# Engine choice left to the order tables for some forty copies, casts and scalings, and the tables made anew, in a fused linear-attention and feed-forward kernel

## The chip, the cores and the metric

The kernel runs on one core of one Trainium2 chip. A core has TensorE (PE in the profile; its weight loads are PEld), VectorE (DVE), ScalarE (ACT), GpSimd (POOL) and SyncE (SP), which only issues DMAs here. The metric is the device time of one execution in microseconds (us), lower is better.

## The reference

Blockwise linear attention with a decay per head, and behind it a feed-forward layer with an activation of its own. B, H, S, D = 4, 8, 768, 64.

```python
for b in range(nb):                                   # blocks of 64 positions
    intra = einsum('bhic,bhjc->bhij', qb, kb) * Dmask  # lam ** (i - j), causal
    intra = einsum('bhij,bhjd->bhid', intra, vb)
    inter = einsum('bhid,bhde->bhie', qb * lam_pow, kv_state)
    out[:, :, sl] = intra + inter
    kv_state = lam_block * kv_state + einsum('bhsd,bhse->bhde', kb * rev_pow, vb)
...
x = out.transpose(0, 2, 1, 3).reshape(3072, 512)
h = x @ w_in                                          # 512 x 2048
g = h + sin(alpha * h) ** 2 / (alpha + 1e-9)
result = g @ w_out                                    # 2048 x 512
```

## The kernel before

The attention works on 24 blocks of 128 positions (six to a batch), the feed-forward layer on six chunks c of 512 tokens, four blocks each. All matmuls are in bf16.

**Attention of a block s.** `scale_block` multiplies q by powers of lam (lines L462 and L472 of the profile) and k (L480, L492), and casts v to bf16 (L486, L495). `piece_Q`, `piece_K` and `piece_T` transpose q and k on PE by `ident` into PSUM, and a copy brings them to `qkT` (L516, L539, L543, L571); from block 12 on, SP transposes by DMA instead. `part_S` makes the scores (L612), and DVE multiplies them by the mask into `Sm` (L623). `part_Z` adds the block's k'v to the running state in bank 7 (L648, L656), which is cast to `Zd` or `Zc` (L666, L672). `part_O`, or `piece_P` and `piece_I` in the first four blocks, make the output in PSUM (L694, L707, L716, L759, L779), and a cast writes it to `xT` (L726, L739). `piece_G` joins the scores of one block with the output and state of the block before.

**Feed-forward of a chunk.** `unit_A` (and `unit_A2`, for two parts of half a chunk) makes one of 16 parts m of h in a PSUM bank (L822, L856); ACT takes the sine into `t16` (L832, L866); ACT or POOL squares it into `u16` (L836, L837; L870, L871); DVE adds it to h with 1/alpha into `gT` (L839, L874), which frees the bank. From chunk 2 on, parts rotate through banks 4, 5 and 6. In chunks 0 and 1 `unit_B` multiplies gT by w_out (L887), and an osb copy (L901) goes before the store. In chunks 2 to 5 the second product goes by seven products instead of eight (`unit_P`, L975): `weight_sums` make sums of quarters of w_out once (L930), `token_sums` sums of quarters of gT for each chunk (L953), and `finish` combines the products (copies into `kept`, L1012; sums L1015 and L1021).

**The head.** SP loads lam, q, k and v of the first four blocks, then the first quarter of w_in (`ws`). POOL's queue loads the rest of w_in (`w1`) and w_out, once the second v block has landed. Meanwhile DVE, POOL and ACT make the exponents, `identf`, `ident` and the masks; POOL also clears `Zd` (L427). PE runs unused matmuls (`spin`, L1134 of the profile) on a constant tile until there is something to do.

**The order.** Nothing runs by the order in which the code stands. Each call of `op` records one operation with a number, what it reads and writes, and its engine, or a choice of engines. `_Plan.ORDER` holds, for each engine, the numbers in the order in which that engine issues them; in PE's table a pair (n, columns) stands for n unused matmuls. `_settle` gives an operation to the engine whose table names it:

```python
o = self.ops[table[0]]
assert o.given == e or e in (x[0] for x in o.given)
...
o.eng = e
```

`emit` then puts in the semaphore waits. Two operations of one engine need a wait between them only if `_ordered` says no: if one reads what the other wrote, on any engine but PE. So the tables alone set the order of every engine's queue, and the durations written in the code have no effect on what is issued.

Operations that the prediction names by number: 47 and 48, the casts of the first two v blocks; in the stretch of the sums, the parts gT of chunk 2, part 13, and of chunk 3, part 10.

Of the kernel before, what the change touches and what calls it, by code (L numbers as in the profile page):

```python
# [6 lines left out]
ACTF = mybir.ActivationFunctionType  # L7
# [6 lines left out]
class _Op:  # L14


    def __init__(self, eng, emit, dur, reads, writes, dma, after, issue, lat, runs=64):
        self.eng, self.emit, self.dur = eng, emit, dur
        self.given = eng
        self.issue, self.lat, self.runs = issue, lat, runs  # L20
        self.lag = 2.9 if eng == "POOL" else 2.0
        self.lead = 0
        self.reads, self.writes, self.dma = reads, writes, dma
        self.port = False
        self.after = after
        self.deps = set()
        self.needed = False
        self.count = None
        self.start = None
        self.done = None  # L30
        self.knows = None


class _Plan:
# [17 lines left out]
        ),  # L52
        "ACT": (
# [16 lines left out]
        ),  # L70
        "DVE": (
# [14 lines left out]
        ),  # L86
        "POOL": (
# [7 lines left out]
        ),  # L95
# [67 lines left out]
    def _ordered(d, o):  # L163


        if d.eng != o.eng or d.dma is not None:
            return False
        return d.eng == "PE" or not (set(d.writes) & set(o.reads) or set(d.reads) & set(o.writes))

    def emit(self):  # L170
        order = self._settle()
        place = {o: i for i, o in enumerate(order)}
        for o in order:
            for d in o.deps:
                d.needed = d.needed or not self._ordered(d, o)
# [33 lines left out]
def bass_lightning_attn__then__act_snake_kernel(  # L209
# [35 lines left out]
    QD = ((0, 0), (0, 2), (1, 0), (1, 2))  # L245

    es = contextlib.ExitStack()
    with es:
# [55 lines left out]
        def _(_unused_eng):  # L304
# [76 lines left out]
            def cast_w1_first():  # L381
                for lo in (0, 256):
                    op("DVE",
# [3 lines left out]
            def load_w2(i, after):  # L387
# [26 lines left out]
                fill=1.0, base=0, channel_multiplier=1), 0.5, ["identf"], ["identf", "select"])  # L414
            op("DVE", lambda e: e.tensor_copy(ident[:, :], identf[:, :]), 0.2, ["identf"], ["ident"])
            op("DVE", lambda e: e.memset(maskf[:, :, :], 1.0), 0.3, writes=[("maskf", i) for i in range(3)])
            for i in range(3):
                t, ks = (4, 2) if i < 2 else (2, 1)
                for r in ((0, 64), (64, 128)) if i < 2 else ((0, 128),):
                    op("POOL", lambda e, i=i, r=r, t=t, ks=ks: e.affine_select(  # L420
# [825 lines left out]
```

## Time and profile before

| | |
|---|---|
| three runs | 210.68, 211.11, 211.37 us; median 211.11 |
| span of the profiled execution | 209.8 us |
| around the span (median less span) | 1.3 us |
| PE, DVE, ACT, POOL busy | 97, 76, 76, 60% of the span |
| DMA | 33.35 MB, mean 159 GB/s |
| first product with w_in (L856) starts | 18.99 us |

The profiled execution has no other time of its own on its page than its span. Busy shares count an engine's time from the start to the end of its instructions; the ends of matmuls are modelled. The chain is the work that ended last, followed back from the end. In the windows the first number of an engine is its busy time in the stretch, the (x) its instructions, then come the granted clock of PE (1.00 is full), the DMA share and GB/s.

### The profile page before, as it was taken

To read this page: it belongs to the slowest core of one execution; us is meant where nothing else is said; L and a number is where in the kernel's file an instruction comes from. 1 tells how busy PE (TensorE), PEld (TensorE's weight loads), DVE (VectorE), ACT (ScalarE), POOL (GpSimd) and SP (SyncE) were. 2 spreads that over 40 slices of the span, in tenths; PEclk is the share of its full clock that TensorE was granted. 3 is DMA by queue.
4 is the path that set the end of the run, shared out by engine and by line. 5 is a ranking of instruction groups with operands and counts; after the bars stand their busy time and mean duration, and the time that the engine had idled before them with its cause. 6 is when DMAs were issued, how large, how long until landed. Compare 5 with 4: busy or idle time off the path is not lost.

```text
span 209.8 us, 4867 instructions
## 1 busy us (share of the span) xinstructions
PE 203.5 (97%) x1975; PEld 134.3 (64%) x1975; DVE 160.3 (76%) x266; ACT 158.7 (76%) x294; POOL 126.9 (60%) x130
## 2 busy tenths in 40 slices
PE   7979999999999999999998999999999999999995
PEld 6847444457677776555555667766667765666894
DVE  4884557563999866868899799889698699777643
ACT  4949995968998989999997887787963889568210
POOL 7075354994469578679885392944581957378300
DMA  4999999999998999999999920190000004000514
GB/s 141 310 318 232 206 213 237 246 229 256 220 264 205 227 245 230 223 233 196 246 271 228 213 53 0 33 271 2 3 0 3 0 23 179 3 0 0 200 40 163
DMA packets 78998, 33.35 MB, mean 159 GB/s; under 512 B 55408, under 2 KB 76160, under 8 KB 78976
## 3 DMA queue, kind: packets, MB, share of 16 engines
q1 hardware_dynamic: 73744, 27.14, 56.2%
q0 software_dynamic: 3696, 3.67, 10.5%
q10 hardware_dynamic: 1536, 2.24, 3.3%
q8 instruction: 15, 0.25, 0.5%
q14 instruction: 7, 0.06, 0.1%
HBM read 27.28 MB, written 6.29 MB: 160 GB/s over the span
## 4 chain that ended last, share of the span: by engine, by line
PE 83%; DVE 6%; DMA 3%; SPq 3%; ACT 2%; issue 1%
PE bank L822 27%; PE bank L975 22%; PE bank L887 13%; PE bank L856 10%; DMA v<-in_v_dram 3%; PE bank L716 3%; SPq L315 3%; PE bank L612 3%; DVE gT L839 2%; PE bank L694 1%; DVE Sm L623 1%; PE bank L511 1%; PE bank L656 1%; DVE w L930 1%; PE bank L534 1%; PE bank L707 1%
## 5 line engine op out<-in xcount | busy, mean ns | idle before, releaser
L822 PE MATMUL bank<-xT,w 128*128 128x512 bf16 x296 | 70.5, 379 | 0.0
L839 DVE SCALAR_TENSOR_TENSOR gT<-u,rinv,bank 128x512 bf16<-128x512 bf16 x74 | 53.6, 742 | 18.2 <-ACT u L836 12.5
L832 ACT ACTIVATE t<-bank,alpha 128x512 bf16<-128x512 f32 x74 | 50.0, 684 | 21.0 <-PE bank L822 20.5
L822 PEld LDWEIGHTS bank<-xT,w 128*128 128x128 bf16 x296 | 28.3, 98 | 28.4 <-DVE gT L839 0.4
L836 ACT ACTIVATE u<-t 128x512 bf16<-128x512 bf16 x59 | 36.5, 628 | 1.3
L837 POOL TENSOR_TENSOR u<-t 128x512 bf16<-128x512 bf16 x15 | 16.0, 1066 | 34.1 <-ACT t L832 30.5
L953 POOL TENSOR_TENSOR gT<-gT 128x512 bf16<-128x512 bf16 x24 | 27.8, 1172 | 11.2 <-DVE Xs L953 6.0
L623 DVE TENSOR_TENSOR Sm<-bank,mask 128x1024 bf16<-128x1024 f32 x24 | 29.1, 1218 | 4.3 <-PE bank L648 1.8
L887 PE MATMUL bank<-w,gT 128*128 128x512 bf16 x128 | 31.4, 380 | 0.0
L874 DVE SCALAR_TENSOR_TENSOR gT<-u,rinv,bank 128x256 bf16<-128x256 bf16 x44 | 18.8, 476 | 7.8 <-ACT u L870 6.1
L472 POOL TENSOR_TENSOR qk<-q,Lq 128x512 bf16<-128x512 f32 x20 | 21.2, 1075 | 2.8 <-DMA q<-in_q_dram 2.8
L856 PE MATMUL bank<-xT,w 128*128 128x256 bf16 x176 | 22.2, 273 | 0.0
L492 POOL TENSOR_TENSOR qk<-k,Lk 128x512 bf16<-128x512 f32 x20 | 20.9, 1053 | 0.6 <-DMA k<-in_k_dram 0.6
L866 ACT ACTIVATE t<-bank,alpha 128x256 bf16<-128x256 f32 x44 | 18.9, 476 | 2.0 <-PE bank L856 1.5
L887 PEld LDWEIGHTS bank<-w,gT 128*128 128x128 bf16 x128 | 11.7, 98 | 12.2
L856 PEld LDWEIGHTS bank<-xT,w 128*128 128x128 bf16 x176 | 16.4, 98 | 3.5 <-issue 0.3
L953 POOL TENSOR_TENSOR Xs<-gT 128x512 bf16<-128x512 bf16 x13 | 16.1, 1235 | 1.5 <-DVE gT L839 1.4
L975 PE MATMUL bank<-w,gT 128*128 128x256 bf16 (+1 forms) x136 | 16.3, 266 | 0.0
L975 PE MATMUL bank<-w,Xs 128*128 128x256 bf16 (+1 forms) x136 | 16.0, 267 | 0.1
L975 PE MATMUL bank<-ws,gT 128*128 128x256 bf16 x128 | 15.8, 273 | 0.0
L975 PEld LDWEIGHTS bank<-w,gT 128*128 128x128 bf16 x136 | 12.6, 98 | 3.2
L975 PEld LDWEIGHTS bank<-w,Xs 128*128 128x128 bf16 x136 | 12.4, 98 | 2.8 <-DVE osb L1021 0.3
(101 smaller groups left out, 276.0 us busy)
## 6 DMA issues: line engine op xcount, KB each, us to landing
q<-in_q_dram SPq DMA_DIRECT2D x12, 512.0 KB, 6.2
k<-in_k_dram SPq DMA_DIRECT2D x24, 256.0 KB, 5.5
v<-in_v_dram SPq DMA_DIRECT2D x24, 256.0 KB, 5.4
out_dram<-osb SPq DMA_DIRECT2D x14, 256.0 KB, 2.5
w<-in_moe_w_out_dram POOLq DMA_DIRECT2D x4, 512.0 KB, 11.4
w<-in_moe_w_in_dram POOLq DMA_DIRECT2D x3, 512.0 KB, 9.0
ws<-in_moe_w_in_dram SPq DMA_DIRECT2D x2, 512.0 KB, 7.5
out_dram<-osb ACTq DMA_DIRECT2D x8, 128.0 KB, 4.0
```

The lines of the kernel that those rows point to most:

```text
L472: lambda e, a=a: e.tensor_tensor(qk2[:, j:j + 2, 4 * a:4 * a + 4, :], q32[:, jq, 4 * a:4 * a + 4, :, :].rearrange("p h t d -> p t h d"), b ...
L492: lambda e: e.tensor_tensor(qk2[:, j, H:2 * H, :], block32(k32, jl), lk, ALU.mult), 1.05,
L623: op("DVE", lambda e: e.tensor_tensor(Sm[js][:, :, :], banks[:, 512 * b0:512 * b0 + 1024].rearrange("p (c i) -> p c i", i=128), bass.AP(ma ...
L822: ins = e.matmul(ps[hb][:, c0:c1], w1[:, kc, 128 * m:128 * (m + 1)], xT[x][:, kc, c0:c1], start=(kc == 0 and c0 == lo), stop=(kc == NKC - ...
L832: op("ACT", lambda e: e.activation(t16[ju][:, w], ps[hb][:, w], ACTF.Sin, scale=alpha[:, m:m + 1]), 0.69 if hi - lo == TCH else 0.475, [ba ...
L836: lambda e: (e.activation(u16[ju][:, w], t16[ju][:, w], ACTF.Square) if e is nc.scalar else e.tensor_tensor(u16[ju][:, w], t16[ju][:, w], ...
L839: op("DVE", lambda e: e.scalar_tensor_tensor(out=gT[g][:, m, w], in0=u16[ju][:, w], scalar=rinv[:, m:m + 1], in1=ps[hb][:, w], op0=ALU.mul ...
L856: ins = e.matmul(ps[hb][:, 256 * i:256 * i + 256], w1[:, kc, 128 * (m + i):128 * (m + i + 1)], xT[x][:, kc, lo:lo + 256], start=(kc == 0 a ...
L866: op("ACT", lambda e, i=i: e.activation(t16[ju][:, 256 * i:256 * i + 256], ps[hb][:, 256 * i:256 * i + 256], ACTF.Sin, scale=alpha[:, m + ...
L887: ins = e.matmul(ps[ob][:, w], gT[g][:, m, 128 * s4:128 * (s4 + 1)], w2[:, m, w], start=(m == 0), stop=(m == NM - 1),)
L953: e.tensor_tensor(dst, in0, in1, alu), 0, rd, wr))
L975: ins = e.matmul(ps[ob][:, lo + d0:lo + d1], lhs, rhs[:, d0:d1], start=first and p == 0, stop=(p == NM // 2 - 1), skip_group_check=True)
```

## The change

Four edits.

1. Operations that had a fixed engine, or a choice of two, now name a set: `AD` is ACT or DVE, `DP` is DVE or POOL, `ADP` all three. These are the scalings of q and k, the v casts, the copies to qkT, the casts to Zd and xT, the first w1 casts, the osb copies and two copies in `finish`.
2. All five tables are made anew. On the way 35 more operations leave ACT than come to it (291 to 256), DVE goes from 266 to 292 and POOL from 119 to 128. SP's loads and the order of PE's units change too.
3. The unused matmuls are others: before the first transposes 42 of 112 columns and 30 of 128 become 7 of 512, 24 of 128, 2 of 512 and 41 of 128; later ones, of 128 and 512 columns between the first real matmuls, become 6 of 128 in one place.
4. POOL's small fills lose the shared key `select` that kept them in order. Instead, two neighbours in POOL's table get a wait between them if one of them is a mask fill over 64 partitions. And the four Exp instructions read `warm`, so that they follow the first one.

```diff
@@ class _Op
+        self.some = False
+        self.strict = None
@@ _Plan.ORDER, the first entries
         "PE": (
-            (42,112), 39, (30,128), 57, (11,128), 55, (1,128), 53, (1,128), 59, (8,128), 61, (1,512), 62,
-            (3,512), 65, 67, 69, 70, (3,512), 73, 75, 78, 80, 82, 85, (2,512), 87, 90, 91, 93, 124, 130, 140,
+            (6, 512), (1, 512), (24, 128), (2, 512), (9, 128), (32, 128), 59, 57, 39, 55, 53, 61, 62, 67, 69,
+            70, 65, 78, 75, (6, 128), 73, 82, 80, 85, 87, 90, 93, 91, 124, 130, 140, 136, 147, 144, 151, 159,
...
         "POOL": (
-            12, 13, 14, 18, 15, 21, 22, 24, 25, 27, 29, 30, 50, 47, 48, 102, 103, 52, 105, 106, 104, 142, 107,
+            21, 14, 24, 12, 13, 15, 41, 22, 25, 18, 27, 45, 50, 47, 48, 29, 30, 102, 52, 103, 105, 104, 106,
...
         "SP": (
-            0, 2, 3, 4, 5, 6, 7, 8, 9, 10, 11, 96, 97, 112, 109, 110, 111, 113, 114, 116, 115, 117, 119, 118,
+            0, 2, 3, 5, 4, 6, 7, 9, 8, 10, 11, 96, 97, 109, 110, 112, 111, 113, 114, 115, 117, 116, 118, 122,
...
@@ _ordered, emit
-        if d.eng != o.eng or d.dma is not None:
+        if d.eng != o.eng or d.dma is not None or d is o.strict:
             return False
...
+        last = None
+        for o in order:
+            if o.eng == "POOL" and o.dma is None:
+                if last is not None and (o.some or last.some):
+                    o.strict = last
+                    o.deps.add(last)
+                last = o
@@ constants
-    QD = ((0, 0), (0, 2), (1, 0), (1, 2))
+    AD = (("ACT", 0, 0), ("DVE", 0, 0))
+    DP = (("DVE", 0, 0), ("POOL", 0, 0))
+    ADP = (("ACT", 0, 0), ("DVE", 0, 0), ("POOL", 0, 0))
@@ scale_block (q, k, v; the same in four more places)
-                    ported(op("POOL",
+                    ported(op(DP,
                        lambda e, a=a: e.tensor_tensor(
                            qk2[:, j:j + 2, 4 * a:4 * a + 4, :],
...
-                ported(op((("ACT", 0.62, 0.0), ("POOL", 1.05, 0.3)) if s > 11 else "ACT",
+                ported(op(ADP,
                    lambda e: (e.copy if e is nc.scalar else e.tensor_copy)(v2[:, j, :, :], block32(v32, jl)), 0.62,
@@ part_Z
-                        op("ACT" if s < NP else (("ACT", 0.36, 0.0), ("DVE", 0.43, 0.0)), lambda e, r=r: ...
+                        op(AD, lambda e, r=r: ...
@@ unit_B, finish
-                op("ACT", lambda e: e.copy(osb[jo][:, w], ps[ob][:, w]), 0.59, [bank(ob)], parts)
+                op(AD, lambda e: (e.copy if e is nc.scalar else e.tensor_copy)(osb[jo][:, w], ps[ob][:, w]), 0.59, [bank(ob)], parts)
```

More of the change, by code (lines that the diff above doesn't have):

```diff
@@ L382, in cast_w1_first @@
                 for lo in (0, 256):
-                    op("DVE",
+                    op(AD,
                        lambda e, lo=lo: (e.copy if e is nc.scalar else e.tensor_copy)(
@@ L413, in _ @@
                 out=identf[:, :], in_=identf[:, :], pattern=[[-1, 128]], compare_op=ALU.not_equal,
-                fill=1.0, base=0, channel_multiplier=1), 0.5, ["identf"], ["identf", "select"])
+                fill=1.0, base=0, channel_multiplier=1), 0.5, ["identf"], ["identf"])
             op("DVE", lambda e: e.tensor_copy(ident[:, :], identf[:, :]), 0.2, ["identf"], ["ident"])
@@ L419, in _ @@
                 for r in ((0, 64), (64, 128)) if i < 2 else ((0, 128),):
-                    op("POOL", lambda e, i=i, r=r, t=t, ks=ks: e.affine_select(
+                    part = op("POOL", lambda e, i=i, r=r, t=t, ks=ks: e.affine_select(
                         out=maskf[r[0]:r[1], i, :], in_=maskf[r[0]:r[1], i, :], pattern=[[1, t], [t, 128 // t]],
                         compare_op=ALU.is_ge, fill=0.0, base=-i if i < 2 else 0, channel_multiplier=-ks), 0.3,
-                       [("maskf", i), "select"], [("maskf", i), "select"])
+                       [("maskf", i)], [("maskf", i)])
+                    part.some = i < 2
                 op("DVE", lambda e, i=i: e.tensor_copy(mask[i][:, :], maskf[:, i, :]), 0.2, [("maskf", i)], [("mask", i)])
             for i in range(2):
-                op("POOL", lambda e, i=i: e.memset(Zd[i][:, :, :], 0.0), 0.5, writes=[("Zd", i, 0), ("Zd", i, 1), "select"])
+                op("POOL", lambda e, i=i: e.memset(Zd[i][:, :, :], 0.0), 0.5, writes=[("Zd", i, 0), ("Zd", i, 1)])
             op("ACT", lambda e: e.activation(lnlam[:, :], lam_bc[:, :], ACTF.Ln), 0.25, ["lam"], ["lnlam"])
@@ L434, in _ @@
             op("ACT", lambda e: e.activation(Lq[:, NB:NB + 4, :], lnL[:, 2 * NB:2 * NB + 4, :], ACTF.Exp), 0.2,
-               ["lnL"], ["Lq4"])
+               ["lnL", "warm"], ["Lq4"])
             op("ACT", lambda e: e.activation(Lp[:, :, :], lnL[:, 0:NP, :], ACTF.Exp, scale=-1.0), 0.2,
-               ["lnL"], ["Lp"])
+               ["lnL", "warm"], ["Lp"])
             op("ACT", lambda e: e.activation(Lk[:, :, :], lnL[:, NB:2 * NB, :], ACTF.Exp, scale=-1.0), 0.3,
-               ["lnL"], ["Lk"])
-            op("ACT", lambda e: e.activation(Lq[:, 0:NB, :], lnL[:, 0:NB, :], ACTF.Exp), 0.2, ["lnL"], ["Lq"])
+               ["lnL", "warm"], ["Lk"])
+            op("ACT", lambda e: e.activation(Lq[:, 0:NB, :], lnL[:, 0:NB, :], ACTF.Exp), 0.2, ["lnL", "warm"], ["Lq"])
             op("ACT", lambda e: e.activation(warm[:, :], lnlam[:, 0:1], ACTF.Sin, scale=0.0), 1.5,
@@ L446, in _ @@
             op("ACT", lambda e: e.copy(alpha[:, :], ps[4][:, 0:NM]), 0.2, [bank(4), "warm"], ["alpha"])
-            def QE(s, a):
-                return "DVE" if (s, a) in QD else "POOL"
             def ported(o):
@@ L460, in scale_block @@
                         for t in (0, 2):
-                            ported(op(QE(a, t),
+                            ported(op(DP,
                                lambda e, a=a, t=t: e.tensor_tensor(
@@ L467, in scale_block @@
                                    ALU.mult),
-                               1.05 if QE(a, t) == "POOL" else 0.64,
+                               0.64,
                                [("q32", a, 0), ("q32", a, 1), "Lq4"], [("q2", t, a), ("q2", t + 1, a)]))
                 for a in range(2) if s % 2 == 0 and s > 2 else ():
-                    ported(op("POOL",
+                    ported(op(DP,
                        lambda e, a=a: e.tensor_tensor(
@@ L478, in scale_block @@
                     for a in range(2) if s % 2 == 0 else ():
-                        eng, dur = ("DVE", 0.68) if s + a < 3 else ("POOL", 1.05)
-                        ported(op(eng, lambda e, a=a: e.tensor_tensor(
+                        ported(op(DP, lambda e, a=a: e.tensor_tensor(
                             qk2[:, j:j + 2, H + 4 * a:H + 4 * a + 4, :],
@@ L483, in scale_block @@
                             bass.AP(Lp, n * H + 4 * a, [[NP * H, 128], [H, 2], [1, 4], [0, D]]), ALU.mult),
-                           dur, [("k32", jl + a), "Lp"], [("k2", j, a), ("k2", j + 1, a)]))
+                           0.68, [("k32", jl + a), "Lp"], [("k2", j, a), ("k2", j + 1, a)]))
                     for a in range(2) if s % 2 == 0 else ():
-                        ported(op("ACT" if s and not a else "POOL", lambda e, a=a: (e.copy if e is nc.scalar else e.tensor_copy)(
+                        ported(op(ADP, lambda e, a=a: (e.copy if e is nc.scalar else e.tensor_copy)(
                             v2[:, j:j + 2, 4 * a:4 * a + 4, :],
@@ L490, in scale_block @@
                     return
-                ported(op("POOL",
+                ported(op(DP,
                    lambda e: e.tensor_tensor(qk2[:, j, H:2 * H, :], block32(k32, jl), lk, ALU.mult), 1.05,
                    [("k32", jl), "Lk"], [("k2", j, 0), ("k2", j, 1)]))
-                ported(op((("ACT", 0.62, 0.0), ("POOL", 1.05, 0.3)) if s > 11 else "ACT",
+                ported(op(ADP,
                    lambda e: (e.copy if e is nc.scalar else e.tensor_copy)(v2[:, j, :, :], block32(v32, jl)), 0.62,
@@ L538, in piece_Q @@
                     if len(tbs) == 2:
-                        op("ACT", lambda e, a=a: e.copy(qkT[:, jt:jt + 2, 2 * a:2 * a + 2, :], tps[a]),
+                        op(AD, lambda e, a=a: (e.copy if e is nc.scalar else e.tensor_copy)(
+                            qkT[:, jt:jt + 2, 2 * a:2 * a + 2, :], tps[a]),
                            0.59, [bank(tbs[a])], [("qT", jt, a), ("qT", jt + 1, a)])
@@ L569, in piece_K @@
                 for t in range(2):
-                    op("ACT" if s else (("DVE", 0.43, 0.0), ("ACT", 0.6, 0.0)),
+                    op(AD,
                        lambda e, t=t: (e.copy if e is nc.scalar else e.tensor_copy)(qkT[:, jt + t, 4:8, :], tps[t]),
@@ L665, in then @@
                         r = slice(64 * h, 64 * h + 64)
-                        op("ACT" if s < NP else (("ACT", 0.36, 0.0), ("DVE", 0.43, 0.0)), lambda e, r=r: (e.copy if e is nc.scalar else e.tensor_copy)(
+                        op(AD, lambda e, r=r: (e.copy if e is nc.scalar else e.tensor_copy)(
                             Zd[s % 2][r, :, r], ps[ZB][r, :].rearrange("p (a b) -> p a b", b=128)[:, :, r] if s < NB else
@@ L737, in evict @@
                 P.lead = -20
-                for eng, a0, a1, dur in (("ACT", 0, 2, 0.46), ("DVE", 2, 4, 0.4)) if len(obs) > 1 else (("ACT", 0, 4, 0.74),):
-                    op(eng, lambda e, a0=a0, a1=a1: (e.copy if e is nc.scalar else e.tensor_copy)(
+                for a0, a1 in ((0, 2), (2, 4)) if len(obs) > 1 else ((0, 4),):
+                    op(AD, lambda e, a0=a0, a1=a1: (e.copy if e is nc.scalar else e.tensor_copy)(
                         xT[c % RX][:, a0:a1, BL * i4:BL * (i4 + 1)].rearrange("p a (u x t) -> p a u t x", u=nq // 2, t=2),
                         ps[obs[a0 // 2 % len(obs)]][:, 128 * a0:128 * a1].rearrange(
-                            "p (a u t x) -> p a u t x", a=a1 - a0, u=nq // 2, t=2)), dur,
+                            "p (a u t x) -> p a u t x", a=a1 - a0, u=nq // 2, t=2)), 0.4,
                        [bank(obs[a0 // 2 % len(obs)])], [("xT", c % RX, i4, a) for a in range(a0, a1)])
@@ L1011, in finish @@
                 if i in (1, 3):
-                    op("ACT", lambda e: e.copy(c1 if i == 1 else ny, got), 0.59 if n == 2 else 0.37, [bank(ob)], kc if i == 1 else kn)
+                    op(AD, lambda e: (e.copy if e is nc.scalar else e.tensor_copy)(c1 if i == 1 else ny, got), 0.59, [bank(ob)], kc if i == 1 else kn)
                     return
```

103 rows, old and new, of the table ORDER are left out of this document.

## The prediction

> **What bounds the kernel now.** I read the page first: the busy shares, then the chain that ended last.
>
> ```profile
> span 209.8 us, 4867 instructions
> PE 203.5 (97%) x1975; PEld 134.3 (64%) x1975; DVE 160.3 (76%) x266; ACT 158.7 (76%) x294; POOL 126.9 (60%) x130
> PE 83%; DVE 6%; DMA 3%; SPq 3%; ACT 2%; issue 1%
> ```
>
> TensorE is the bound: it is on the chain for 83% of the span. The change leaves all its useful matmuls alone, so it can only win or lose where TensorE waits. Next I asked the windows where that is. The columns are the engines' busy us in each stretch.
>
> ```profile
> 105.00:110.00 5.00, 5.00 (x29) 2.65 (x27) 5.00 (x6) 4.58 (x9) 4.42 (x4) 1.00 1.23 274
> 110.00:115.00 5.00, 4.44 (x53) 2.97 (x51) 4.87 (x8) 3.85 (x7) 3.19 (x3) 1.00 1.04 228
> 120.00:125.00 5.00, 4.89 (x47) 3.21 (x46) 5.00 (x8) 4.03 (x8) 5.00 (x6) 1.00 0.38 71
> ```
>
> Between 20 and 205 us these last two are the only windows of 5 us in which PE is not 5.00 busy: 0.56 + 0.11 = 0.67 us. In both DVE is full (4.87 and 5.00), and so it is just before (5.00). The ends of matmuls are modelled, so shorter gaps are hidden in "5.00"; still, most of the chip time behind 20 us is already TensorE's work, and no reordering can give much there. The chain in order of time shows who held TensorE at 112 us:
>
> ```profile
> 104.76 1.23 DVE Sm L623
> 105.99 1.31 DVE gT L839 x2
> 107.30 1.19 DVE Xs L953
> 108.49 0.66 DVE gT L839
> 109.15 1.88 DVE w L930
> 111.05 0.43 DVE Zd L666
> ...
> 112.32 0.40 PE bank L694 x4
> ```
>
> For 7.5 us the chain is DVE's queue alone. It is the stretch in which weight sums (L930) and token sums (L953) are added to the ordinary work. DVE, not ACT, is what is nearly late today.
>
> The chain's first part is the head: the load of v, then ACT's short evictions one behind the other, up to the first product with w_in (L856).
>
> ```profile
> 4.16 1.13 POOL L427 MEMSET Zd<- 128x512 bf16 x2
> 5.84 2.50 DVE L462 TENSOR_TENSOR qk<-q,Lq 128x512 bf16<-128x512 f32 x4 [1.01 <-ACT Lq L434]
> 7.20 0.40 PE L534 MATMUL bank<-ident,qk 128*128 128x128 bf16 x4 [0.18 <-DVE qk L462]
> 13.61 0.62 POOL L486 CAST v<-v 128x512 bf16<-128x512 f32 x1 [1.31 <-DMA v<-in_v_dram]
> 14.29 0.62 PE L648 MATMUL bank<-v,qk 64*128 64x128 bf16 x8 [0.90 <-POOL v L486]
> 15.01 0.75 ACT L666 CAST Zd<-bank 64x256 bf16<-64x256 f32 x2
> 18.99 2.07 PE L856 MATMUL bank<-xT,w 128*128 128x256 bf16 x16
> ```
>
> **The change part by part.** *Which engine does what.* By the two sets of tables, ACT goes from 291 to 256 instructions (table loads apart), DVE from 266 to 292, POOL from 119 to 128. These rows price the moves:
>
> ```profile
> L472 POOL TENSOR_TENSOR qk<-q,Lq 128x512 bf16<-128x512 f32 x20 | 21.2, 1075 | 2.8 <-DMA q<-in_q_dram 2.8
> L462 DVE TENSOR_TENSOR qk<-q,Lq 128x512 bf16<-128x512 f32 x4 | 2.5, 688 | 1.0 <-ACT Lq L434 1.0
> L495 ACT CAST v<-v 128x512 bf16<-128x512 f32 x19 | 11.6, 618 | 0.0
> L901 ACT COPY osb<-bank 128x512 f32<-128x512 f32 x8 | 4.7, 589 | 0.1
> L1021 DVE TENSOR_TENSOR osb<-bank,kept 128x512 f32<-128x512 f32 x6 | 4.1, 684 | 0.5 <-PE bank L975 0.5
> L839 DVE SCALAR_TENSOR_TENSOR gT<-u,rinv,bank 128x512 bf16<-128x512 bf16 x74 | 53.6, 742 | 18.2 <-ACT u L836 12.5 <-POOL u L837 5.2
> ```
>
> Ten q and k scalings go POOL to DVE: 10 x 0.69 = 6.9 us onto DVE, 10 x 1.05 off POOL. Eighteen v casts leave or change places, twelve of them ACT to POOL (0.62 each) and six onto DVE; no row has that cast on DVE, so I bound it from below by half a scaling (0.35) and above by a whole one (0.69), and take 0.4: 2.4 us. Eight output and kept copies go ACT to DVE; by L1021 as the nearest read of PSUM on DVE they cost 0.68 each, less for two halves, about 5 us. Eighteen squares go ACT to POOL and fourteen come back. Small evictions mostly exchange, net about 3 us onto DVE; weight sums move three from DVE to POOL (-2 us). DVE ends some 14 us heavier (168 to 182 us of summed durations), ACT some 20 lighter, POOL 8 heavier. So the change relieves the engine that TensorE does not wait for and loads the one that it does wait for. ACT's relief I cost at nothing: the chain gives ACT 2%, nearly all in the head.
>
> *What DVE and POOL share.* Rows of the timeline, DVE first and then POOL, the durations of one form (min, median, max), and line L953 alone in one window:
>
> ```profile
> 107.22 1.27 DVE L953 TENSOR_TENSOR Xs<-gT 128x512 bf16<-128x512 bf16 x1
> 109.07 1.95 DVE L930 TENSOR_TENSOR w<-w 128x1024 bf16<-128x1024 bf16 x1
> ...
> 107.05 1.16 POOL L953 TENSOR_TENSOR gT<-gT 128x512 bf16<-128x512 bf16 x1
> 108.17 2.30 POOL L930 TENSOR_TENSOR w<-w 128x1024 bf16<-128x1024 bf16 x1
> ...
> L953 DVE TENSOR_TENSOR gT<-gT x24: 409/418/1372, 98.2 to 200.2; 128x512 bf16<-128x512 bf16 x24
> 97.50:128.20 30.70, 7.15 (x11) 8.31 (x7) 1.00 0.92 193
> ```
>
> A token sum takes DVE 0.41 us at best and up to 1.37. The one that started at 107.22 ended 0.28 us after POOL's (107.05 + 1.16 = 108.21): it stood still until POOL was through, then ran. The weight sum at 109.07 did the same behind POOL's 2.30. The last row is line L953 alone: eleven DVE sums took 7.15 us where 11 x 0.41 = 4.5 would do. [...]
>
> *The stretch of the sums.* One product of four matmuls is 3.45 / 4 = 0.86 us:
>
> ```profile
> 35.53 3.45 PE bank L822 x16
> ```
>
> I compare the same two DVE instructions in both orders: gT of chunk 2, part 13, and gT of chunk 3, part 10. Before, 28 DVE instructions lie between them (17.9 us), with 21.6 us of TensorE work between their matmuls. After, 39 lie there (25.1 us): 13 of L839, 11 token sums, 3 masks, 3 weight sums, 3 scalings or v casts, 3 Zd, 3 others; and TensorE has 13 + 4 + 8 products of about 0.87 and some 3.4 us of attention by the starts of its matmuls, 25.1 us. DVE instructions overlap a little (two of L839 take 1.31 on the chain, not 2 x 0.74), 0.09 each: 25.1 - 39 x 0.09 = 21.6 us, so 3.5 us are over for waiting. Seventeen of the 39 read two SBUF tensors or cast from SBUF. At the stretch of the rows above, (7.15 - 4.5 + 1.27) over 14 sums = 0.28 each, they lose 17 x 0.28 = 4.8 us: DVE is 1.3 us late. The low end is 0 (POOL happens to be elsewhere). The high end: POOL is busy three quarters of the time and a DVE sum meets the middle of a 1.16 us one, 0.75 x 0.58 x 17 = 7.4, so 3.9 late. I take 1.3, the row's, against the 0.6 lost there before: net +0.7, from -0.6 to +3.3. Behind each late gT stands a bank of the three (4, 5, 6) that the next products rotate through, so DVE's lateness reaches TensorE within about two products.
>
> *The 55 to 75 us stretch.* [...] Cost +0.2, from 0 to 1.
>
> *The head.* SP loads the second half of v before the first, but POOL casts the first half first (ops 47, 48). Both now wait for the fourth load, which let the row at 13.61 go. So the second cast ends at 13.61 + 2 x 0.62 = 14.85 and the first state product (L648) starts 0.56 later than 14.29. Behind the casts POOL clears Zd (0.6 each, 1.13 for both, at 4.16 before): done at 15.4 and 15.9, and the Zd casts that began at 15.01 need the first at 15.4: no more than 0.1 beyond the 0.56. From there ACT has the same Zd pair to do twice, but half the third pair and one xT go to DVE. The last waits are ACT's xT evictions, as before. I take +0.6 (18.99 to 19.6), from -0.4 (the evictions moved to DVE shorten ACT's row) to +1.5. On the way there TensorE has 74 unused matmuls in a row where it had 72 before its first transpose, and identf is made on POOL behind a q scaling of 1.05, so the first transposes come at about 9 us and not 7.20. [...] The POOL queue's weight loads slide too, by 1.8 us behind casts and clears; before them SP no longer sends a k block, so the engines have the same bytes to move less that block: 0, at most +1.
>
> *POOL's own waits* between neighbours that touch half the partitions, and Exp's wait on the warm-up, are some 0.1 us each before 9 us, under the loads. *The tail* from the last product on is the same chain: 0.
>
> **Sum.** +0.6 + 0.7 + 0.2 = +1.5 us. The page's span is 209.8 and the median of the three runs 211.1, so 1.3 us lie around the span; the forecast is 211.1 + 1.5 = 212.6 us. I hold 0.3%, 0.6 us, to be the least that a measurement of this kernel tells from no change.
>
> **Rivals.**
> *DVE fits, the order is simply better (faster).* If POOL's sums happen to lie beside DVE's one-input work, the 0.67 us at 110 to 125 go and the head gains its 0.4: 211.1 - 0.67 - 0.4 = 210.0. For it: only 0.67 us was lost with DVE full, so the orders do fit. [...] Chance 0.21.
> *A wash.* The head costs 0.6 and the sums give 0.6 back: 211.1. Chance 0.15.
> [...] The high ends: 3.3 at the sums, 1 at 55 to 75 us, 1 in the head: 216.4. [...] Chance 0.16.
> *TensorE slow again in the head.* The first 42 unused matmuls (112 columns) took longer per column than the next 30 (128 columns):
>
> ```profile
> 1.52 3.55 PE L1134 MATMUL bank<-Xs 128*128 128x112 bf16 x42 [1.52 <-DVE Xs L410]
> 5.16 1.85 PE L1134 MATMUL bank<-Xs 128*128 128x128 bf16 x30
> ```
>
> That is 84.5 ns against 61.7, or 0.75 ns a column against 0.48. Nearly all unused matmuls now lie before 9 us; between 9 and 19 only six are left, so TensorE idles more. If it fell back for as long as at the start, 3.55 us of work would take 1.3 us more: 212.6 + 1.3 = 213.9. [...] The gaps I see are under 2 us. Chance 0.08.
>
> The forecast itself has 0.40.
>
> **How the numbers follow.** Faster takes the first rival, 0.21, and a little of the wash's lower half, 0.22. Same is most of the wash and the forecast's low edge, 0.16. Slower is the rest, 0.62. The range leaves out the best tenth and the worst tenth: 210.2 to 216.0.
>
> **What would show it.** Right: PE below 5.00 in several windows between 98 and 130 us, the chain there on DVE L839 and on sums whose durations pass 1 us; first L856 at 19.6; ACT near 138 us busy, DVE near 175. The term for the head is wrong if L856 starts before 19; the term for the sums is wrong if PE stays 5.00 through 100 to 130 with DVE full. [...]

## The result, and the profile after

| | before | after |
|---|---|---|
| median, us | 211.17 (210.68 to 211.37, 4 runs) | 227.91 (227.64 to 228.63, 4 runs) |
| ratio, 95% interval | | 1.0802 (1.0771 to 1.0833) |
| span of the profiled execution, us | 209.8 | 225.9 |
| first product with w_in (L856, now L864) starts | 18.99 | 24.74 |

Slower, as forecast, but by 16.7 us and not by 1.5, outside the range. Medians are over all executions; a ratio leaves out those more than 1.5% above the fastest of the same kernel. Lines of the kernel after stand 7 to 11 further down than before (L839 is L847, L953 is L961, L930 is L938).

The page of after, the lines that answer to those shown of before, and the granted clock in 40 slices:

```profile
span 225.9 us, 4816 instructions
PE 206.6 (91%) x1927; PEld 134.8 (60%) x1953; DVE 184.0 (81%) x292; ACT 141.7 (63%) x259; POOL 139.8 (62%) x139
PEclk9985799999999999999999999999999999999999
PE 58%; DVE 26%; ACT 8%; POOL 2%; issue 2%; DMA 1%; ACTq 0%; DVEq 0%; POOLq 0%
```

TensorE is on the chain for 58% instead of 83%, DVE for 26% instead of 6%. The granted clock dips in the third to fifth slices (0.8, 0.5, 0.7), most in the fourth. The windows show both kinds of loss; the columns are as in the prediction's:

```profile
10.00:15.00 5.00, 2.64 (x44) 1.91 (x45) 4.97 (x11) 1.64 (x4) 4.42 (x6) 1.00 1.17 307
15.00:20.00 5.00, 4.81 (x78) 3.66 (x76) 3.89 (x4) 2.32 (x5) 4.57 (x7) 0.51 1.01 187
20.00:25.00 5.00, 5.00 (x90) 3.94 (x89) 1.94 (x4) 3.09 (x7) 0.00 (x0) 0.50 1.17 188
120.00:125.00 5.00, 4.45 (x50) 2.84 (x48) 5.00 (x6) 4.03 (x8) 5.00 (x4) 1.00 1.05 235
125.00:130.00 5.00, 2.79 (x17) 1.49 (x16) 4.91 (x6) 2.34 (x6) 5.00 (x5) 1.00 1.01 165
130.00:135.00 5.00, 3.82 (x24) 2.19 (x24) 5.00 (x8) 2.68 (x5) 4.31 (x4) 1.00 0.29 65
```

First loss: for about 10 us, from 15.2 to 25.4 us, TensorE ran at half its clock (granted clock 0.50 in that stretch), and the first product with w_in came 24.74 - 18.99 = 5.75 us late. Second loss: behind that product the kernel needs 225.9 - 24.7 = 201.2 us, before 209.8 - 19.0 = 190.8, so 10.4 us more. By the starts of the matmuls TensorE stands for 0.44 and 0.89 us at 45 and 46 us, 0.89 at 103, 0.71, 2.08, 0.82, 0.28 and 1.64 between 122 and 136, 1.12 at 146, 0.99 at 157 and some smaller ones. The chain in order of time at the longest of these; then the timeline of DVE and of POOL at the same place; then DVE's groups (us in all and mean ns):

```profile
120.94 1.45 DVE w L938
122.39 0.66 DVE gT L847
123.05 0.64 DVE gT L961
123.69 2.53 DVE w L938
126.21 0.66 DVE gT L847
```

```profile
123.61 2.60 DVE L938 TENSOR_TENSOR w<-w 128x1024 bf16<-128x1024 bf16 x1
...
123.37 2.30 POOL L938 TENSOR_TENSOR w<-w 128x1024 bf16<-128x1024 bf16 x1
125.63 1.49 POOL L499 TENSOR_TENSOR qk<-k,Lk 128x512 bf16<-128x512 f32 x1
```

```profile
L961 DVE TENSOR_TENSOR gT<-gT 128x512 bf16<-128x512 bf16 x25 | 17.9, 724 | 0.1
L961 DVE TENSOR_TENSOR Xs<-gT 128x512 bf16<-128x512 bf16 x19 | 12.0, 637 | 0.1
L480 DVE TENSOR_TENSOR qk<-q,Lq 128x512 bf16<-128x512 f32 x8 | 7.2, 902 | 0.0
L938 DVE TENSOR_TENSOR w<-w 128x1024 bf16<-128x1024 bf16 x3 | 4.8, 1603 | 0.0
```

A weight sum that takes DVE 0.68 us (the shortest of the three here, and their mean in e5) took 2.60: POOL's, begun 0.24 earlier, ended at 125.67, and DVE was through 0.54 later. The gT behind it (126.21) frees the bank that TensorE waits for. Over the four groups DVE spends 41.9 us; at 0.41 for a token sum, 0.69 for a scaling and 0.68 for a weight sum it would be 25.6.

### The profile page after: what moved, and what is told of

Read it like the earlier page. It is cut to its first block, busy times and chain, and to the rows that moved or that the text cites. A ratio compares the mean times of both kernels' runs of the same rounds, so it can differ in the third digit from the quotient of the medians.

```text
span 225.9 us, 4816 instructions
## 1 busy us (share of the span) xinstructions
PE 206.6 (91%) x1927; PEld 134.8 (60%) x1953; DVE 184.0 (81%) x292; ACT 141.7 (63%) x259; POOL 139.8 (62%) x139
## 3 DMA queue, kind: packets, MB, share of 16 engines
q0 software_dynamic: 3696, 3.67, 10.4%
q10 hardware_dynamic: 1536, 2.24, 3.5%
## 4 chain that ended last, share of the span: by engine, by line
PE 58%; DVE 26%; ACT 8%; POOL 2%; issue 2%; DMA 1%; ACTq 0%; DVEq 0%; POOLq 0%
PE bank L830 16%; PE bank L983 12%; PE bank L895 9%; PE bank L864 9%; DVE gT L847 8%; DVE gT L961 3%; ACT t L840 3%; DVE Xs L961 3%; PE bank L620 3%; ACT u L844 3%; PE bank L724 2%; DVE Sm L631 2%; DVE qk L480 2%; DVE w L938 2%; PE bank L656 2%
## 5 line engine op out<-in xcount | busy, mean ns | idle before, releaser
L830 PE MATMUL bank<-xT,w 128*128 128x512 bf16 x280 | 69.0, 380 | 7.9 <-DVE gT L847 6.5
L847 DVE SCALAR_TENSOR_TENSOR gT<-u,rinv,bank 128x512 bf16<-128x512 bf16 x74 | 53.3, 740 | 11.8 <-ACT u L844 7.2
L830 PEld LDWEIGHTS bank<-xT,w 128*128 128x128 bf16 x296 | 27.3, 98 | 37.7 <-DVE gT L847 10.5
L845 POOL TENSOR_TENSOR u<-t 128x512 bf16<-128x512 bf16 x22 | 23.1, 1058 | 25.4 <-ACT t L840 23.5
L844 ACT ACTIVATE u<-t 128x512 bf16<-128x512 bf16 x52 | 32.4, 629 | 2.9 <-DVE gT L847 0.8
L961 POOL TENSOR_TENSOR gT<-gT 128x512 bf16<-128x512 bf16 x23 | 29.0, 1273 | 7.9 <-DVE Xs L961 4.0
L895 PE MATMUL bank<-w,gT 128*128 128x512 bf16 x118 | 29.7, 379 | 1.5 <-ACT qkT L523 0.7
L499 POOL TENSOR_TENSOR qk<-k,Lk 128x512 bf16<-128x512 f32 x18 | 20.3, 1136 | 4.9 <-PE bank L664 4.9
L864 PE MATMUL bank<-xT,w 128*128 128x256 bf16 x176 | 22.6, 276 | 0.0
L961 POOL TENSOR_TENSOR Xs<-gT 128x512 bf16<-128x512 bf16 x13 | 16.2, 1248 | 6.8 <-DVE gT L847 6.8
L895 PEld LDWEIGHTS bank<-w,gT 128*128 128x128 bf16 x128 | 11.9, 98 | 12.5 <-DMA w<-in_moe_w_out_dram 0.6
L864 PEld LDWEIGHTS bank<-xT,w 128*128 128x128 bf16 x176 | 16.6, 99 | 3.4 <-DVE qk L480 0.4
L879 POOL TENSOR_TENSOR u<-t 128x512 bf16<-128x512 bf16 x4 | 4.2, 1038 | 22.5 <-ACT t L874 22.5
L961 DVE TENSOR_TENSOR gT<-gT 128x512 bf16<-128x512 bf16 x25 | 17.9, 724 | 0.1
L983 PE MATMUL bank<-w,gT 128*128 128x256 bf16 (+1 forms) x136 | 15.5, 266 | 0.0
```

What stands on the lines that cost most here:

```text
L499: lambda e: e.tensor_tensor(qk2[:, j, H:2 * H, :], block32(k32, jl), lk, ALU.mult), 1.05,
L830: ins = e.matmul(ps[hb][:, c0:c1], w1[:, kc, 128 * m:128 * (m + 1)], xT[x][:, kc, c0:c1], start=(kc == 0 and c0 == lo), stop=(kc == NKC - ...
L844: lambda e: (e.activation(u16[ju][:, w], t16[ju][:, w], ACTF.Square) if e is nc.scalar else e.tensor_tensor(u16[ju][:, w], t16[ju][:, w], ...
L845: e.tensor_tensor(u16[ju][:, w], t16[ju][:, w], t16[ju][:, w], ALU.mult)), 0,
L847: op("DVE", lambda e: e.scalar_tensor_tensor(out=gT[g][:, m, w], in0=u16[ju][:, w], scalar=rinv[:, m:m + 1], in1=ps[hb][:, w], op0=ALU.mul ...
L864: ins = e.matmul(ps[hb][:, 256 * i:256 * i + 256], w1[:, kc, 128 * (m + i):128 * (m + i + 1)], xT[x][:, kc, lo:lo + 256], start=(kc == 0 a ...
```

## The experiments

**Where: the head or the rest?** Theories: the two losses are separate and add; or the rest is only late because the head is. The changed code took the tables of before, then the head (all up to the first product with w_in) of one kernel and the rest of the other.

```diff
 ORDER = {
-    tables of after
+    e1: tables of before
+    e2: head of before, then what is left of the tables of after
+    e3: head of after, then what is left of the tables of before
```

> The changed code with the five order tables of the kernel before, unused matmuls included. If the loss is in the tables alone, as both theories have it, this is 211.1 us within 0.6. If the lost ordering key of POOL's fills or the Exp's wait on the warm-up cost something, it is above 212.

> Everything up to the first product with w_in in the order and on the engines of before (with its unused matmuls), everything behind it as in the changed kernel. Granted clock 1.00 throughout. If the two stretches add, the head's 5.8 us go and about 10.4 are left over before: 222 us. If the rest was only late because the head was (loads, clock), it is below 216. If the rest has slack that had swallowed part of the head's delay, it is above 223.

> The opposite: the head of the changed kernel, the rest as before. If the two stretches add: 211.1 + 5.8 = 217 us, with the granted clock at half for about 10 us from 15 us on. If the rest takes the delay back: 213 to 215.

e1: 211.72 in one run; in twelve more:

> The changed code with the tables of before, as in the first run, now timed in rounds. If the code edits cost something: 211.5 to 211.9 and a ratio over 1.002. If the first run was a chance value: within 0.2% of before.

210.94, ratio 1.0005 (0.9991 to 1.0018): the code edits cost nothing, the tables are all of it. e2: 224.63, ratio 1.0643 (1.0584 to 1.0703), 2.6 over the forecast; a stall of 2.32 us at 31 us, where the two orders meet, is its own. The stalls of the rest stand as in after, in the same places and sizes (2.08, 0.82, 0.28, 1.64, 1.12, 0.99), although the clock was full (1.00) in the profiled execution: the second loss is the rest's own. e3 gave no single time: four executions from 216.7 to 227.4 us. The fastest is near the 217 that adding would give, the others are not, so the sum isn't tested there. Its longest execution is the one in the profile, and this is what DVE and then POOL did in it from 38 to 49 us:

```profile
39.55 9.49 DVE L939 TENSOR_TENSOR Ta<-w 128x1024 bf16<-128x1024 bf16 x1
48.96 1.39 DVE L848 SCALAR_TENSOR_TENSOR gT<-u,rinv,bank 128x512 bf16<-128x512 bf16 x2
...
38.30 1.05 POOL L500 TENSOR_TENSOR qk<-k,Lk 128x512 bf16<-128x512 f32 x1
39.31 2.04 POOL L481 TENSOR_TENSOR qk<-q,Lq 128x512 bf16<-128x512 f32 x2
41.31 1.03 POOL L500 TENSOR_TENSOR qk<-k,Lk 128x512 bf16<-128x512 f32 x1
42.31 4.17 POOL L939 TENSOR_TENSOR ws<-w 128x1024 bf16<-128x1024 bf16 x2
46.45 2.03 POOL L481 TENSOR_TENSOR qk<-q,Lq 128x512 bf16<-128x512 f32 x2
48.45 2.48 POOL L500 TENSOR_TENSOR qk<-k,Lk 128x512 bf16<-128x512 f32 x2
```

One weight sum of 0.7 us stood for 9.49 us, behind seven POOL instructions without a gap, until 48.48, and TensorE stood for 6.83 us. Six of POOL's instructions ended without letting it in; at the seventh end it went, though POOL did not pause there: its next two scalings, begun at 48.45, took 2.48 us where two take 2.1. What made the seventh end different is not shown. It is a single event: in the twenty profiles here 383 sums, scalings and v casts of DVE's from 18 us on waited 0.1 us or more for POOL, and all the others went at the first end of a POOL instruction. The weight sum and its neighbours in this order are before's; only the head is different.

**The clock.** Theories: TensorE's idling made the chip halve its clock; or the half clock lies beside other waits.

```diff
-    (32, 128), 59, 57, 39, 55, 53, 61, 62, 67, 69, 70, 65, 78, ...
+    (47, 128), 59, 57, 39, 55, 53, 61, (3, 512), 62, (4, 512), 67, (1, 512), 69, 70, 65, (1, 512), 78, ...
```

> The changed kernel with more unused matmuls where TensorE idled between 9 and 16 us: 15 of 128 columns ahead of the first transposes, then 3, 4, 1 and 1 of 512 columns between the transposes and scores. Theory clock (TensorE's idling made the chip halve its clock): granted clock 1.00 throughout, first product with w_in near 21.5 us instead of 24.74, total about 225. Theory late start (the head waits for POOL and DVE anyway, the half clock lies beside other waits): first product no earlier than 23.7, total 227 or more. If the clock is halved all the same, idling is not its cause.

225.41, ratio 1.0672 (1.0637 to 1.0706), so 2.5 us less than after. The windows of e4, and from its timeline the first product with w_in:

```profile
10.00:15.00 5.00, 3.92 (x48) 2.31 (x49) 4.97 (x10) 1.64 (x4) 4.68 (x8) 1.00 1.17 311
15.00:20.00 5.00, 4.52 (x121) 3.40 (x119) 4.76 (x5) 3.16 (x8) 4.02 (x6) 1.00 1.03 201
20.00:25.00 5.00, 4.85 (x70) 3.57 (x72) 2.42 (x4) 3.99 (x10) 0.00 (x0) 1.00 1.17 177
```

```profile
21.79 1.48 PE L867 MATMUL bank<-xT,w 128*128 128x256 bf16 x12
```

The same window of before:

```profile
10.00:15.00 5.00, 3.92 (x85) 2.21 (x86) 4.35 (x6) 2.20 (x5) 2.99 (x4) 1.00 1.16 310
```

Theory clock holds: with TensorE 3.92 busy from 10 to 15 us (2.64 in after, 3.92 before) the clock stays full, and the first product comes 2.95 us earlier. It still comes 2.8 us later than before. In this window 3.65 us busy (e2) also left the clock full, 1.00, and 2.98 (e13, mean granted clock 0.970) and 2.43 (e3, 0.67 and 0.50 in the next two windows) did not. Where between 2.98 and 3.65 the limit lies, and whether the sum of the gaps or the longest of them sets it, no run here shows.

**The late start of the head.** In after, the chain in order of time from 6 to 13 us goes through POOL and DVE:

```profile
6.33 1.55 POOL qk L470
7.94 0.66 POOL maskf L430
8.65 0.64 POOL maskf L430
...
10.05 1.01 DVE mask L435
11.06 1.47 DVE qk L487
```

POOL makes a scaling of q in 1.55 us beside DVE's, then two mask fills that wait for each other, then identf; a cast of a mask takes DVE 1.01 us while POOL scales k, where such a cast took 0.23 in before (at 2.96 us). Three runs, all with unused matmuls added. From here on the expectations speak of a theory lock (e13 and e16 call it port): DVE's instructions with two SBUF inputs stand still while POOL reads SBUF. The names stand for that alone.

```diff
 e11   POOL: identf ahead of the scaling 41; DVE: ident ahead of its scalings
 e12   the scalings 41 (q) and 45 (k) from POOL to DVE, as before
 e15   as e12, with no unused matmuls added ahead of the first transposes
```

> The changed kernel with the added unused matmuls (225.4 us, first product with w_in at 21.79, first transposes at 10.1), and identf made ahead of the q scaling on POOL and cast to ident ahead of the q scalings on DVE. If the identity holds the head: first transposes near 8.2 us and the first product with w_in near 20, total about 224. If POOL's two scalings of k hold it (2.05 us from 9.93, DVE's scaling standing still until they are through), the transposes start early and the first product stays at 21.5 or later, total 225.

> The changed kernel with the added unused matmuls, and the two scalings of the head that the change moved to POOL (one of q, one of k) back on DVE. Theory lock in the head: DVE's scalings fall from 0.93 and 1.17 us to 0.69, though DVE has two more, first transposes near 9 us, first product with w_in near 20, total about 223.5. If DVE is simply short of time there, the first product stays at 21.8 or comes later.

> The changed kernel with the two scalings of the head back on DVE, and unused matmuls added only between the first transposes and scores (3, 4, 1 and 1 of 512 columns), none ahead of the transposes. First transposes near 9.2 us, first product with w_in near 19.6, granted clock 1.00; if the head's delay reaches the end one to one, the total is 227.9 - 5.1 = 222.8. If the rest is held by its own stalls whatever the head does, 224 or more.

e11 took 223.86 (ratio 1.0596, 1.0559 to 1.0633), but its first transposes came at 10.94: the unused matmuls ahead of them were still running, so it doesn't test the identity. e12: 225.54, first product at 20.38, transposes at 9.95, again behind unused matmuls. The timeline of e12 (DVE), and of e15 (TensorE):

```profile
6.24 2.50 DVE L473 TENSOR_TENSOR qk<-q,Lq 128x512 bf16<-128x512 f32 x4 [1.93 <-ACT Lq L448]
```

```profile
19.82 1.92 PE L867 MATMUL bank<-xT,w 128*128 128x256 bf16 x16
```

Four scalings of q on DVE take 2.50 us, where in after three of them beside POOL's one took 2.84. With the two scalings back and TensorE kept busy, the first product starts at 19.82: 4.9 of the 5.75 us are mended. The totals do not show it one to one. e12 starts the product 1.4 us ahead of e4 and is no faster (225.54 against 225.41). e15's time is 225.08 (222.62 to 226.52): the profiled execution took 222.62 at full clock, the other three ran at a mean granted clock of 0.992. The clock is not all of that spread, for e12 ran from 223.45 to 225.72 at full clock; the rest of it is not explained.

**The rest: POOL's reads or the load?** Theory lock, as above; theory load: DVE has more to do and gT comes late. Four runs of different kinds. The copies and casts of e7 read PSUM; in after DVE's eight casts of that kind to xT took 0.71 to 0.74 us each, so none of them waited for POOL.

```diff
 e5, e6 (tables of after, of before): POOL's sums and scalings behind the head
-    e.tensor_tensor(dst, in0, in1, alu)
+    e.memset(dst, 0.0) if e is nc.gpsimd else e.tensor_tensor(dst, in0, in1, alu)
 e7   tables of before, 23 copies and casts out of PSUM from ACT to DVE
 e8   tables of before, 10 scalings and 6 v casts from POOL and ACT to DVE
```

> The changed kernel, but POOL's weight sums, token sums and q and k scalings behind the head write a zero instead of the sum or product: the same instruction slots, waits and tiles, no reads of SBUF (this part of the computation is left out). POOL's squares and casts stay. Theory lock (DVE's two-input instructions stand still while POOL reads SBUF): the token sums on DVE fall from 0.69 us mean to near 0.42, the weight sums from 1.60 to 0.70, the stalls of TensorE between 100 and 200 us (0.90, 0.71, 2.08, 0.82, 0.28, 1.64, 1.12, 0.99, 0.54 and smaller, 10.7 in sum) mostly go, total about 218. Theory load (DVE has 14 us more to do, in an order that makes gT late): durations as they were, total 226 or more.

> The same with the tables of before: the control. Theory lock: before loses little to it, at most the 0.73 + 0.32 us of stalls at 111 and 123 us: 210.5 to 211.7. If POOL's shorter instructions by themselves bring time, this shows how much: then it is below 210.

> [...] Theory load: DVE at 171 us busy is late for gT, total 215 or more. Theory lock: DVE has the room, 211 to 213.

> The order of before, with the ten scalings of q and k that the change moves from POOL to DVE, and its six v casts, moved to DVE alone: 10 x 0.69 + 6 x 0.4 = 9.3 us more on DVE if nothing held them. Theory lock: their mean is well over 0.8 us, they take 13 us or more, and the total is above that of the copies: 214 to 218. Theory load: less than the copies cost, and their mean near 0.69. A gain would say that POOL's relief (10 x 1.05 us) is worth more than DVE's load.

e5: 219.73, ratio 1.0397 (1.0373 to 1.0420), 8.2 us less than after. DVE's groups in e5 (all through the one line of the helper, L465):

```profile
L465 DVE TENSOR_TENSOR gT<-gT 128x512 bf16<-128x512 bf16 x25 | 11.8, 483 | 0.1
L465 DVE TENSOR_TENSOR Xs<-gT 128x512 bf16<-128x512 bf16 x19 | 8.4, 452 | 0.1
L465 DVE TENSOR_TENSOR qk<-q,Lq 128x512 bf16<-128x512 f32 x8 | 5.5, 684 | 0.0
L465 DVE TENSOR_TENSOR w<-w 128x1024 bf16<-128x1024 bf16 x3 | 2.0, 682 | 0.0
```

27.7 us where after had 41.9, and of the stalls behind 100 us only 0.78 at 126 is left; ahead of it in the chain stands a token sum of 1.20 us behind one of POOL's squares, which e5 leaves as they are. e6: 210.48, ratio 0.9961 (0.9947 to 0.9976): in before's order the same edit is worth 0.7 us. The edit also makes POOL's instructions shorter (a memset takes 0.52 us, a scaling 1.05) and POOL less busy (87.0 us, in after 139.8). That this is no large part of the 8.2 is shown by e6 for before's order only; in after, POOL's own work stands on the chain behind the head in one place, two squares of 2.05 us at 163. e7: 214.81, ratio 1.0164 (1.0144 to 1.0184); DVE rises to 171.8 us and the load costs 3.6, more than theory lock allowed (213) and a little less than theory load asked (215). e8: 224.31, ratio 1.0580 (1.0515 to 1.0644), from fewer instructions:

```profile
L482 DVE TENSOR_TENSOR qk<-q,Lq 128x512 bf16<-128x512 f32 x8 | 9.1, 1136 | 0.0
L504 DVE CAST v<-v 128x512 bf16<-128x512 f32 x6 | 5.1, 853 | 0.0
```

These are DVE's scalings and casts in e8: 1.14 us for a scaling that takes 0.69 alone. (e8 also ran at a mean granted clock of 0.985 to 0.992, so a part of its 13 us is clock.) Load counts on this order; sharing counts more.

**Undone from the other side.** Theory lock in a narrower form: the sixteen sharers moved are what does it. Sharers are DVE's instructions that read two SBUF tensors or cast from SBUF.

```diff
 e13   tables of after, the 16 sharers of e8 back to POOL and ACT
 e16   tables of after, the 23 copies and casts of e7 back to ACT
```

> The changed kernel with 16 instructions put back where they were before: behind the head, ten scalings of q and k from DVE to POOL, and of the six v casts five to ACT and one to POOL. Theory port (the sharers bring the loss): the stalls at 46, 102, 134, 145 and 156 us (0.89, 0.90, 1.64, 1.12, 0.99), where DVE was in a scaling or a cast, go; total 222 to 224. Theory load: DVE has some 9.3 us of work less, at the price that the copies showed on before (3.6 us for 12.4), a gain of 2.7: 225.2.

> [...] Theory port: the sharers still stand still as long as before, total 225.5 to 227.5. Theory load: DVE is no longer late, 222 or less.

e16: 227.72, ratio 1.0797 (1.0768 to 1.0825): 23 instructions less on DVE, and nothing gained. Load does not explain after. But e13 is 226.43 (1.0732, 1.0698 to 1.0767), not 222 to 224: the narrow theory falls. DVE's weight sums still took 1.46 us and its token sums 0.67 and 0.70, with new stalls of 1.89 us at 119 and 1.25 at 127. The scalings that went back to POOL are not what holds DVE up there: of 14.1 us that e13's sharers wait for POOL, its scalings account for 0.6, its token sums for 8.0, its squares for 3.6 and its weight sum for 1.9. What counts, by e5 and e13 together, is not which sixteen moved but how often POOL is reading when DVE's turn comes, and that is a property of the whole order.

Both known causes away at once, head as before and no reads by POOL:

> The head as before, the rest as after, and POOL's weight sums, token sums and scalings behind the head write zeros (this part is left out). Both known causes are away. If they are all there is, what is left over before is the one stall of 2.3 us at the seam that the run without this edit showed at 31 us: 212.5 to 214. If the order itself costs more, it is 216 or above.

214.63, ratio 1.0171 (1.0144 to 1.0198), a little above. Its largest stalls are 2.95 us at 31 (where the orders meet) and 0.78 at 122, again behind one of POOL's squares; without them 214.6 - 3.7 = 210.9, before's time. If stalls count one to one, next to nothing is left for the order as such. Against e2, which has the same head, the reads are worth 224.63 - 214.63 = 10.0 us.

**One meeting alone.** One weight sum that DVE stood behind goes from POOL to DVE, so that DVE gets more work and one wait less.

```diff
 e9         after:  "POOL" ... -605 ...   "DVE" ... 603, +605 ...
 e10, e18   before: "POOL" ... -604 ...   "DVE" ... +604, 603 ...   (e10 in the changed code, e18 in its own)
```

> One instruction moved in the changed kernel: the weight sum that POOL makes at 123.4 us for 2.30 us goes to DVE, right behind DVE's own weight sum that stood still behind it (2.60 us at 123.61). Theory load: DVE gets one instruction more of 0.7 us where it is latest, so the total grows to 228.5. [...]

> The same in the order of before: the weight sum that POOL makes at 108.17 us (2.30 us) goes to DVE right ahead of the one that stood still behind it (1.95 us at 109.07). Theory lock: DVE does both in 0.68 + 0.68 us, the stall of 0.73 us at 111.5 goes, 210.3 to 210.8, faster than before by some 0.3%. Theory load: DVE is full there, one more instruction makes it later, 211.5 or more.

> The kernel before with one instruction moved: the weight sum of 2.30 us at 108.17 goes from POOL to DVE. If the blocking at 109 us is what costs the stall of 0.73 us, it shrinks as it did with the changed code (0.98 to 0.59), and the total is 210.3 to 210.9. If DVE's token sums only meet POOL's elsewhere: 211.0 to 211.5.

e9: 226.97, ratio 1.0756 (1.0736 to 1.0776), 0.9 us less than after with one instruction more on DVE, where theory load has it grow. But DVE's two sums did not take twice 0.68 us; they took 2.97. The timeline of e9, DVE's two sums and POOL beside them:

```profile
123.28 2.97 DVE L940 TENSOR_TENSOR w<-w 128x1024 bf16<-128x1024 bf16 x2
...
123.04 1.22 POOL L501 TENSOR_TENSOR qk<-k,Lk 128x512 bf16<-128x512 f32 x1
124.62 1.08 POOL L847 TENSOR_TENSOR u<-t 128x512 bf16<-128x512 bf16 x1 [0.36 <-ACT t L842]
```

POOL's next scaling and square took the place of its weight sum; TensorE's stall of 2.08 us grew to 2.44, and the one of 1.64 at 134 us shrank to 0.49. In before the stall at 111 us is 0.59 us instead of 0.73, which shows nothing, as with the tables of before it was 0.98 in e1 and absent in e17. The kernel became slower, not faster: e10 211.77 (1.0024 to 1.0051), e18 211.73 (1.0026 to 1.0055). DVE's two sums took 2.24 us there, behind a token sum of POOL's. Where the 0.8 us went the two profiles don't show; it stays open. No version here that computes everything beats before.

## Why the prediction was wrong

**The sum.** 16.7 us: 2.5 clock (e4), 8.2 POOL's reads behind the head (e5), 2.8 late start (first product at 21.79 in e4 against 18.99) make 13.5, if a late start reaches the end one to one, which e12 and e15 did not show. The stalls that e5 keeps (0.48 at 33, 0.44 and 0.27 at 46, 0.78 at 126) are 2.0, where before has 1.0 of its own, so 1.0 more; 2.2 are not placed. The terms are not independent either: with the head of before the reads cost 10.0 (e2, e14), not 8.2.

**The head, +0.6 forecast, 5.75 measured.** The sum has no term for TensorE's fewer unused matmuls and for the scaling ahead of identf, and that is the step that failed. The transposes came at 10.11 and not at 9; the scalings of k on POOL then held DVE's cast and scaling; and idling cost the clock. What I did cost came out near: with the scalings back on DVE and TensorE kept busy (e15) the product starts at 19.82, where I had 19.6.

**TensorE slow again: the right rival with a chance of 0.08 and 1.3 us, against 2.5 us measured.** It was set aside because the gaps were "under 2 us". They were, in before (0.90 at the longest, ahead of 14.29) and in after: 0.91, 0.82, 1.12 and 0.32 us between 9 and 15 us. Together they left TensorE 2.64 busy in the 5 us from 10 to 15, and the granted clock was 0.51 and 0.50 in the next two windows; with 3.92 busy (e4) it stayed 1.00. A gap of 2 us was not needed for it.

**The stretch of the sums, +0.7 (at most +3.3) forecast; 5.5 us of stalls measured between 122 and 136, where before has 1.0 in all.** Two steps failed. The size: by the timeline, the 17 sharers of this stretch lost 6.8 us (durations less 0.41, 0.68, 0.66 and 0.37 by form), 0.40 each and not 0.28; my high end took half a token sum of POOL's, 0.58 us, as the usual wait, and behind a weight sum DVE waited 1.93 us. The method: I took 3.5 us of slack off the sum of the waits once, as if slack anywhere paid for a wait anywhere. With 6.8 my count would give 6.8 - 3.5 = 3.3, and TensorE lost 5.5 us. Part of the slack was spent elsewhere: DVE stood idle for 0.49 us at 117.8 and 0.57 at 136.3, on either side of the long waits. As I see it, with banks 4, 5 and 6 in turn, slack ahead of a wait is gone when the wait comes; no run here tests that.

**Outside that stretch** I costed 55 to 75 us (+0.2, a term that no run shows by itself; in after no stall there is over 0.37 us) and nothing else; the other 4.9 of the 10.4 us lie at 45, 103, 146 and 157 us, each of these with a sharer on DVE ahead of the late gT or copy in the chain, and in small ones.

**The high ends, 216.4 with a chance of 0.16,** came nearest, and too low. I priced the waits by their mean, 0.28 us. Over the 64 sharers of the rest the mean wait is 0.30 us, before 0.18 over 50. The mean was the wrong measure: what grew is the number of waits, not their size. In after 30 of the 64 waited 0.1 us or more, 0.62 on average, in before 12 of the 50, 0.72 on average. POOL's squares, to which the prediction gave no price, stand behind 6.2 of after's 18.6 us of waiting and behind none in before. Each of these 42 waits ended 0.28 us (token sums, casts) or 0.55 us (scalings, weight sums) after the end of one POOL instruction. So the loser stood to the end of the POOL instruction that was reading; in e3 one stood through six ends of POOL's instructions, so the end of one instruction is not a sure bound.

**Signs.** PE under 5.00 between 98 and 130 and DVE's sums past 1 us came as described; ACT came to 141.7 busy (138 forecast), DVE to 184 (175): waiting counts as busy there, for without most of POOL's reads (e5) the same instructions keep DVE busy for 170.9.

## What to carry to other kernels

When work moves between DVE and POOL, look in the timeline for what the other engine does at that moment: in all waits here but one, an instruction of DVE's with two SBUF inputs stood for what was left of the POOL instruction then reading, and in the 42 waits of before and after it ended 0.28 us (token sums, casts) or 0.55 us (scalings, weight sums) behind it. Count how many such meetings an order makes, POOL's squares included; a mean over all instructions hides them. Take slack off place by place, at the bank or buffer that the late instruction frees, not over a whole stretch. And unused matmuls in a head are not filler: before taking them out, add up TensorE's idle time over a stretch. Of the 5 us from 10 to 15 it was busy for 2.43 to 2.98 in the runs whose clock fell (e3, after, e13: means of 0.962 to 0.977), and for 3.65 to 3.92 in those that kept 1.00 (e2, before, e4).

## What was not expected of the hardware

Once (e3), a busy POOL held DVE off across instructions: 9.49 us for a 0.7 us sum. In after four gaps of at most 1.12 us in 6 us were enough for 10 us at a granted clock of 0.50; with unused matmuls in them (e4) it stayed 1.00. And some of these kernels have no single time: e3 ran from 216.7 to 227.4 us, e15 from 222.6 to 226.5.
